# Second scores behind the even value product, its maximum ahead of the first scaling, even value rows copied in two parts

## Chip, core and metric

The kernel runs on one core of a Trainium2 chip. The metric is the device time of one execution in microseconds (us); three runs of the kernel before gave 957.9, 959.9 and 960.99, so the median is 959.9 us.

## What is computed

A sequence of 2048 rows of width 640 goes through an attention layer with a recurrent memory and then through a dense layer with a squared ReLU. The part that matters here is the attention. It walks over 64 segments of 32 rows; each segment needs the 8 memory rows that the segment before it left, so the segments can't run side by side:

```python
for s in range(n_seg):                       # 64 segments of 32 rows
    xs = x[:, s * seg_len:(s + 1) * seg_len, :]
    h = jnp.concatenate([mem, xs], axis=1)   # 8 memory rows + 32 rows
    q, k, v = (einsum('btd,dhe->bhte', h, W) for W in (Wq, Wk, Wv))   # 32 heads of 128
    scores = where(mask, einsum('bhqe,bhke->bhqk', q, k) * scale, -1e9)
    o = einsum('bhqk,bhke->bhqe', softmax(scores), v)
    o = einsum('bhte,hed->btd', o, Wo)
    mem = o[:, :M, :]                        # handed to the next segment
    outs.append(o[:, M:, :])
```

Around it stand a layer norm, the residual sums and the dense layer.

## The kernel before

The order of instructions on each engine is written out by hand; nothing is moved by a scheduler. One call of `step` is one segment, some 12 us long. Its order on TensorE (PE in the profile):

- The projections q (first 16 heads), k, q, k (second 16 heads), each 20 matmuls: `proj` (L234), 5 chunks of the 640 inputs times 4 column strips of the array, which run side by side. ScalarE (ACT) evacuates each result into a row tile (L253, L246, L482) and VectorE (DVE) turns it with 32 by 32 block transposes (L258, and L485 in two halves for the second k). GpSimd (POOL) spreads the queries of the memory rows into `qz` (L441, L443).
- `scores(0)` (L495): the memory rows' scores of the first 16 heads, 16 small matmuls into the bank `sm`. `soft1(0)` then takes the maximum on DVE (L501) and the exponential with its sum on ACT (L504, an activation and the reading of its accumulator).
- The value product has two halves of 512 columns, even (`ps0`) and odd (`ps1`). The even one runs in two pieces with `token_scores(0)` (L587) between them; ACT copies it out as 512 columns (L594).
- The odd product's first chunk (4 matmuls, in a bank of the three of the pool `mm`), then `soft2(0)`: reciprocal (L510), a product with the mask `same` (L511) and the scaling into `pm` (L515) on DVE. Then `scores(1)` and `soft1(1)`, the same for the second 16 heads, in the same bank `sm`. Then `soft3`: a transpose on DVE (L526) and four copies into `pB0` (L529), one on DVE, one on ACT, two on POOL.
- The rest of the odd product with `token_scores(1)` between its chunks, its copy by ACT (L608), and `soft2(1)` on DVE: reciprocal, product (L510, L511), the scaling with the mask `own` (L518), and the transpose into `pB1` (L521).
- Pieces of the other projections (`fill`: tail projections of later segments, 8 or 9 pieces of mostly 4 matmuls to a step, each group of 5 in a bank of `mm`) stand between the two value products of the memory rows: `values(0)` (L537, L542; reads `pB0` and the even value columns, writes the PSUM tile `po0`) and `values(1)` (reads `pB1` and the odd columns, writes `po1`).
- The output projection of the memory rows (`wo_rounds`, L270, 64 matmuls into `pw`), evacuated by ACT (L285, L286) and added by DVE (L287), and transposed into `hT` (L380): this is what the next segment's first projection waits for. Beside it run the rest of `fill` and the token values (L421, L426) of the segment before.

The PSUM has eight banks: three for `mm`, one for `chn` (`sm`, `pw`, one k), four for `po0` and `po1`; `potile(h)` hands out the first bank of `po0` or `po1` as a projection tile before the values use it. A tile of `em` (`bufs=1`) holds the exponentials, first those of the first half, then those of the second.

An instruction waits for signals of other engines. Where it and its weight load have to wait for more signals than they carry, a wait instruction of its own stands ahead of them in the engine's queue; the built program's order shows them.

Of the kernel before, what the change touches and what calls it, by code (L numbers as in the profile page):

```python
# [9 lines left out]
ALU = mybir.AluOpType  # L10
AX = mybir.AxisListType
F32 = mybir.dt.float32
BF16 = mybir.dt.bfloat16
# [3 lines left out]
def kernel(  # L17
# [16 lines left out]
    nc = tc.nc  # L34
# [3 lines left out]
    SEG = 32  # L38
    G = 4
    HG = H // G  # L40
# [8 lines left out]
    TL = SEG - HD  # L49
    NK = SEG + M  # L50
# [18 lines left out]
    s1 = ctx.enter_context(tc.tile_pool(name="s1", bufs=1))  # L69
    s2 = ctx.enter_context(tc.tile_pool(name="s2", bufs=2))  # L70
# [5 lines left out]
    wv = wts.tile([128, DC * HE], BF16)  # L76
# [14 lines left out]
    for g in range(G):  # L91
        r = slice(32 * g, 32 * g + 32)
# [4 lines left out]
    pBs = [const.tile([128, G, 2 * SEG], BF16, name="pB%d" % k) for k in range(2)]  # L97
# [43 lines left out]
    for q in range(4):  # L141
        nc.vector.tensor_copy(out=o0[32 * q:32 * q + 32, :].rearrange("m (c f) -> m c f", f=32),
                              in_=mem0[:].rearrange("m (c q f) -> m q c f", q=4, f=32)[:, q])
# [27 lines left out]
    def rows_of(b, sp):  # L171
        at = HD + sp * SEG
        return lambda c: hTs[b % 2][:, c * CW + at:c * CW + at + SEG]
# [50 lines left out]
    def proj(w, by, lhs, n, ps, c0, c1):  # L224

        if by == "columns":
            wr = w[:].rearrange("p (c g j n k e) -> p c n k g j e", c=DC, g=G, n=2, j=4, k=4)
        elif by == "half":
            wr = w[:].rearrange("p (c k j n e) -> p c n k j e", c=DC, k=G, n=2, j=4)
        else:  # L230
            wr = w[:].rearrange("p (c k n f) -> p c n k f", c=DC, k=G, n=2)
        for c in range(c0, c1):
            for k in range(4):
                nc.tensor.matmul(ps[32 * k:32 * k + 32, :], lhsT=lhs(c), rhs=wr[:, c, n, k], start=(c == 0), stop=(c == DC - 1))  # L234

    def mmtile():
        return mm.tile([128, 512], F32, tag="mm", name="ps")

    def potile(h):
        return pop.tile([128, 2, 512], F32, tag="po%d" % h, name="px%d" % h)[:, 0, :]  # L240
# [81 lines left out]
    def tail_units(b, which):  # L322
        w = {"q": wq, "k": wk, "v": wv}[which]
        lhs = lambda c: tail_rows(b, c)
        st = {}

        def unit(n, c):
            def f():
                if c == 0:
                    st[n] = mmtile()  # L330
                proj(w, "columns" if which != "v" else "order", lhs, n, st[n], c, c + 1)
                return (True, lambda: tail_out(b, which, n, st[n][:])) if c == DC - 1 else None
            return f
        return [unit(n, c) for n in range(2) for c in range(DC)]
# [117 lines left out]
    def step(b, sp, v=None):  # L452
        s = b * 4 + sp
        last = s == NS - 1
        lhs = rows_of(b, sp)
        ready = v is not None
        if not ready:
            v = s2.tile([128, EG], BF16, tag="v", name="v")
# [29 lines left out]
        sms, ems, zms = {}, {}, {}  # L488

        def scores(n):  # L490
            sm = chn.tile([128, 512], F32, tag="ch", name="sm")
            for j in range(4):
                for g in range(G):
                    p = n * 16 + g * 4 + j
                    nc.tensor.matmul(sm[32 * g:32 * g + 32, 0:NK], lhsT=qz[:, p, :], rhs=kT[:, p, :],  # L495
                                     start=(j == 0), stop=(j == 3), skip_group_check=True)
            sms[n] = sm

        def soft1(n):
            mx = s2.tile([128, 1], F32, tag="mx", name="mx")  # L500
            nc.vector.tensor_reduce(out=mx[:], in_=sms[n][:, 0:NK], op=ALU.max, axis=AX.X, negate=True)  # L501
            em = s2.tile([128, SEG + NK], BF16, tag="em", name="em", bufs=1)
            zm = s2.tile([128, 1], F32, tag="zm", name="zm")
            nc.scalar.activation(out=em[:, SEG:], in_=sms[n][:, 0:NK], func=ACT.Exp, bias=mx[:, 0:1], scale=1.0,  # L504
                                 accum_out=zm[:])
            ems[n], zms[n] = em, zm

        def soft2(n):
            rm = s2.tile([128, 1], F32, tag="rm", name="rm")
            nc.vector.reciprocal(out=rm[:], in_=zms[n][:])  # L510
            nc.vector.tensor_tensor(out=ems[n][:, 0:SEG].rearrange("p (j k) -> p j k", k=TL),  # L511
                                    in0=ems[n][:, 2 * SEG:].unsqueeze(1).to_broadcast([128, 4, TL]), in1=same[:], op=ALU.mult)
            if n == 0:
                pm = s1.tile([128, HG, TL], BF16, tag="pkt", name="pm")[:].rearrange("p i k -> p (i k)")
                nc.vector.tensor_scalar(out=pm, in0=ems[n][:, 0:2 * SEG], scalar1=rm[:, 0:1], scalar2=None, op0=ALU.mult)  # L515
                return pm
            pm = s1.tile([128, HG, 32], BF16, tag="pk", name="pm")[:].rearrange("p (g a) k -> p g (a k)", g=G)
            nc.vector.scalar_tensor_tensor(out=pm, in0=ems[n][:, 0:2 * SEG].unsqueeze(1).to_broadcast([128, G, 2 * SEG]),  # L518
                                           scalar=rm[:, 0:1], in1=own[:].unsqueeze(2).to_broadcast([128, G, 2 * SEG]),
                                           op0=ALU.mult, op1=ALU.mult)  # L520
            nc.vector.transpose(out=pBs[1][:], in_=pm)  # L521
            return pBs[1]

        def soft3(pm):
            pT = s1.tile([128, 2, 32], BF16, tag="pTt", name="pT")[:].rearrange("p u k -> p (u k)")
            nc.vector.transpose(out=pT, in_=pm)  # L526
            for g, copy in enumerate((nc.vector.tensor_copy, nc.scalar.copy, nc.gpsimd.tensor_copy, nc.gpsimd.tensor_copy)):
                r = slice(32 * g, 32 * g + 32)
                copy(out=pBs[0][r, g], in_=pT[r])  # L529
            return pBs[0]  # L530

        def values(n, pB, po):
            cols = po[:, 0, 0:128]
# [29 lines left out]
        def first_half():  # L563
            if not last:
                scores(0)
                soft1(0)
# [8 lines left out]
        if not ready:  # L575
            ps0 = potile(0)
# [6 lines left out]
        def token_scores(n):  # L583
            skv = view()
            for j in range(4):
                for g in range(G):
                    nc.tensor.matmul(skv[32 * g:32 * g + 32, n * 4 + j, :], lhsT=qT[:, n * 16 + g * 4 + j, :],  # L587
                                     rhs=kT[:, n * 16 + g * 4 + j, :], start=True, stop=True,
                                     skip_group_check=True)

        token_scores(0)
        if not ready:
            proj(wv, "half", lhs, 0, ps0, 2, DC)
            nc.scalar.copy(out=v[:, 0:512], in_=ps0[:])  # L594
            ps1 = mmtile()
            proj(wv, "half", lhs, 1, ps1, 0, 1)
        if not last:
            pm0 = soft2(0)
            scores(1)
            soft1(1)  # L600
            pT0 = soft3(pm0)
        if not ready:
            proj(wv, "half", lhs, 1, ps1, 1, 2)
        token_scores(1)
        if not ready:
            proj(wv, "half", lhs, 1, ps1, 2, DC)
        if not ready:
            nc.scalar.copy(out=v[:, 512:1024], in_=ps1[:])  # L608
        if not last:
            pT1 = soft2(1)  # L610
        def causal(skv):
            nc.vector.tensor_tensor(out=skv[:, :, M:NK], in0=skv[:, :, M:NK],
                                    in1=mask[:].unsqueeze(1).to_broadcast([128, HG, SEG]), op=ALU.add)
# [34 lines left out]
        ek = s1.tile([128, HG, NK], BF16, tag="ek", name="ek")  # L648
# [5 lines left out]
        pkt = s1.tile([128, HG, TL], BF16, tag="pkt", name="pkt")  # L654
# [28 lines left out]
        pTt = s1.tile([128, 2, 32], BF16, tag="pTt", name="pTt")  # L683
# [194 lines left out]
    for b in range(2, NB):  # L878
        for which in "qk":
            u = tail_units(b, which)  # L880
            plan += [(4 * b - 3 + (which == "k"), 4 * b - 5, u[DC * n:DC * n + DC]) for n in range(2)]
    for b in range(10, NB):
        u = tail_units(b, "v")
# [25 lines left out]
    for b in range(NB):  # L909
        for sp in range(4):  # L910
# [34 lines left out]
            if 2 <= e <= NK4 + 1:  # L945
                late.insert(0, (1.15, lambda e=e: prep_stats0(e - 2), b * 4 + sp))
                mid.append(lambda e=e: prep_norm0(e - 2))
            step(b, sp, v0 if b + sp == 0 else None)

    def end_tails():  # L950
# [14 lines left out]
    for t in range(S // NT):  # L965
# [8 lines left out]
        for fc in range(FC):  # L974
# [10 lines left out]
            r = rs_[fc % 4]  # L985
            nc.scalar.activation(out=r[:, 0:w], in_=ps[:, 0:w], func=ACT.Relu, bias=b1f[:, fc:fc + 1], scale=1.0)  # L986
            nc.vector.tensor_tensor(out=f1T[:, fc, 0:w], in0=r[:, 0:w], in1=r[:, 0:w], op=ALU.mult)
            if more and fc >= 1 and (fc - 1) // 3 < NK4:
                k, stage = divmod(fc - 1, 3)
# [30 lines left out]
        for q in range(NK4):  # L1020
# [6 lines left out]
            for hh in range(2):  # L1027
                k = pr + 2 * hh
# [44 lines left out]
```

## Time and profile before

| what | value |
|---|---|
| median of three runs | 959.9 us (957.9 to 960.99) |
| the profiled execution's own time | 956.46 us |
| its span, first to last instruction | 954.6 us, TensorE clock granted 0.998 |
| PE busy | 923.6 us (97%) |
| DVE, ACT, POOL busy | 703.6 (74%), 552.3 (58%), 309.5 (32%) |
| from 100 to 750 us | PE 641.87 of 650.00 us busy |
| chain that ended last | PE 80%, ACT 6%, DVE 5%, DMA 5%, SP queue 2% |

The segments lie between about 60 and 815 us. They repeat closely: measured from one even value copy (L594) to the next, most steps take 11.98 us, and seven take 12.17. A matmul's record has a tail after its last column has gone in (four strips of 512 columns take 0.38 us on record but follow each other every 0.215 us), so a busy PE is not a PE without stalls. A row of the timeline merges instructions of one kind that follow each other; the bracket tells how long the engine was idle before it and what ended that.

### The profile page before, as it was taken

How to read it: one execution, taken by the hardware profiler on the slowest of the kernel's cores; microseconds unless marked ns; L12 is line 12 of the kernel's file. 1: busy time of each engine (PE TensorE's matmuls, PEld its weight loads, DVE VectorE, ACT ScalarE, POOL GpSimd, SP SyncE). 2: the span in 40 equal slices, each digit the busy share in tenths (PEclk: the TensorE clock that was granted, in tenths of full speed). 3: DMA queues.
4: the chain of work that ended last, by engine and by line, in shares of the span. 5: the costliest groups of instructions: out<-in, count | busy, mean ns of one | idle time of the engine just before them, and what ended most of it. 6: DMA issues, size and time to landing. Idle time of an engine off the chain costs nothing.

```text
span 954.6 us, 55984 instructions
## 1 busy us (share of the span) xinstructions
PE 923.6 (97%) x24760; PEld 544.0 (57%) x24760; DVE 703.6 (74%) x2131; ACT 552.3 (58%) x1460; POOL 309.5 (32%) x1002
## 2 busy tenths in 40 slices
PE   5979999999999999999999999999999999999998
PEld 2445555655565656556565656565655555555555
DVE  5168888778877887877877787878787788556632
ACT  2546666666666666666666666666666666523321
POOL 2123333333333333333333333333333333353300
PEclk9999999999999999999999999999999999999999
DMA  9983201010101000100101010101010221633320
GB/s 352 402 265 70 38 18 27 16 30 13 23 20 28 16 21 24 21 25 11 34 17 23 14 31 14 32 12 33 8 32 8 54 43 21 203 108 88 94 56 28
DMA packets 65875, 56.66 MB, mean 59 GB/s; under 512 B 37384, under 2 KB 61712, under 8 KB 63712
## 3 DMA queue, kind: packets, MB, share of 16 engines
q1 hardware_dynamic: 65392, 52.74, 19.6%
q8 instruction: 194, 3.18, 1.4%
q14 instruction: 49, 0.40, 0.1%
q0 software_dynamic: 224, 0.33, 0.1%
q10 hardware_dynamic: 16, 0.01, 0.0%
HBM read 38.37 MB, written 9.44 MB: 50 GB/s over the span
## 4 chain that ended last, share of the span: by engine, by line
PE 80%; ACT 6%; DVE 5%; DMA 5%; SPq 2%; issue 1%; ACTq 0%
PE ps L234 23%; PE pw L270 15%; PE px L234 14%; PE pk L234 7%; PE y L1030 6%; PE ps L978 6%; ACT v L594 3%; PE ps L270 2%; DMA wq<-in_A_Wq_dram 2%; PE po L421 2%; ACT em L504 2%; SPq L151 2%; DVE pm L518 2%; PE po L537 2%; DVE pB L521 2%
## 5 line engine op out<-in xcount | busy, mean ns | idle before, releaser
L234 PEld LDWEIGHTS <-hT 128*32 128x32 bf16 x7680 | 178.9, 96 | 161.2 <-DVE hT L380 24.3
L270 PE MATMUL pw<-wo,oT 128*32 128x320 bf16 x4224 | 157.7, 299 | 2.5 <-DMA wo<-in_A_Wo_dram 1.0
L270 PEld LDWEIGHTS <-oT 128*32 128x32 bf16 x4224 | 120.0, 96 | 22.8 <-issue 3.7
L258 DVE STREAM_TRANSPOSE qT<-row 128x512 bf16<-128x512 bf16 x128 | 89.5, 699 | 44.1 <-ACT row L253 43.7
L234 PE MATMUL ps<-wv,hT 128*32 128x512 bf16 x1260 | 91.9, 377 | 0.0
L649 ACT ACTIVATE ek<-tk 128x320 bf16<-128x320 f32 x64 | 30.1, 470 | 101.9 <-DVE tk L644 101.9
L655 POOL TENSOR_TENSOR pkt<-ek,rk 128x64 bf16<-128x64 bf16 x64 | 18.8, 294 | 212.1 <-ACT otmp L286 176.0
L234 PE MATMUL px<-wv,hT 128*32 128x512 bf16 x1260 | 85.2, 377 | 0.0
L234 PE MATMUL ps<-wq,hT 128*32 128x512 bf16 x1260 | 81.3, 383 | 3.3 <-DVE hT L380 2.8
L234 PE MATMUL ps<-wk,hT 128*32 128x512 bf16 x1280 | 80.0, 379 | 0.0
L234 PE MATMUL px<-wq,hT 128*32 128x512 bf16 x1260 | 78.9, 379 | 0.0
L234 PEld LDWEIGHTS <-hTt 128*32 128x32 bf16 x1920 | 54.4, 97 | 42.2 <-issue 10.1
L234 PE MATMUL pk<-wk,hT 128*32 128x512 bf16 x1240 | 77.7, 379 | 0.0
L986 ACT ACTIVATE wv<-ps,b1f 128x512 bf16<-128x512 f32 (+1 forms) x56 | 37.6, 672 | 67.0 <-PE ps L978 66.5
L432 ACT CAST oT<-po 128x512 bf16<-128x512 f32 x128 | 68.7, 589 | 8.2 <-PE po L426 2.5
L441 POOL COPY qz<-qT 128x96 bf16<-128x96 bf16 x126 | 33.4, 265 | 111.4 <-DVE qT L258 111.4
L285 ACT COPY otmp<-pw 64x96 f32<-64x96 f32 (+2 forms) x129 | 28.8, 223 | 54.0 <-PE pw L270 33.4
L1030 PE MATMUL y<-wq,wk 128*128 128x320 bf16 x416 | 58.9, 299 | 0.2
L482 ACT CAST row<-ps 128x256 bf16<-128x256 f32 x126 | 40.7, 375 | 30.0 <-PE ps L234 29.1
L253 ACT ACTIVATE row<-ps 128x512 bf16<-128x512 f32 x93 | 54.8, 613 | 5.3 <-PE ps L234 4.0
L253 ACT ACTIVATE row<-px 128x512 bf16<-128x512 f32 x63 | 37.6, 597 | 32.2 <-PE px L234 32.2
L537 PEld LDWEIGHTS <-v 128*32 128x32 bf16 x2016 | 34.1, 94 | 34.7 <-issue 15.6
(138 smaller groups left out, 1886.1 us busy)
## 6 DMA issues: line engine op xcount, KB each, us to landing
wv<-in_A_Wv_dram SPq DMA_DIRECT2D x5, 1024.0 KB
wq<-in_A_Wq_dram SPq DMA_DIRECT2D x5, 1024.0 KB
wk<-in_A_Wk_dram SPq DMA_DIRECT2D x5, 1024.0 KB
wo<-in_A_Wo_dram SPq DMA_DIRECT2D x8, 640.0 KB
o_all<-o SPq DMA_DIRECT2D x256, 7.5 KB
vt<-vt_d SPq DMA_DIRECT2D x60, 64.0 KB
xt<-in_A_x_dram SPq DMA_DIRECT2D x19, 160.0 KB
wq<-in_B_w_dram SPq DMA_DIRECT2D x1, 2080.0 KB
```

Source lines behind the costliest of these rows:

```text
L234: nc.tensor.matmul(ps[32 * k:32 * k + 32, :], lhsT=lhs(c), rhs=wr[:, c, n, k], start=(c == 0), stop=(c == DC - 1))
L253: nc.scalar.mul(out=row, in_=ps, mul=scale)
L258: nc.vector.transpose(out=dst[:, n * 16:(n + 1) * 16, 0:32], in_=row.rearrange("p (h e) -> p h e", e=32))
L270: nc.tensor.matmul(pw[32 * j:32 * j + 32, c0:c0 + DH], lhsT=lhs(p), rhs=wov2[:, head(p), ch], start=(h == 0), stop=(h == 15))
L432: nc.scalar.copy(out=oTg[:, gs, :, :, 0:SEG], in_=po[1][h][:, :, 0:256].rearrange("p g (n j q) -> p g n j q", n=2, q=32))
L441: nc.gpsimd.tensor_copy(out=d.rearrange("p a (j f) -> p a j f", j=3)[:, :, :, 0:M], in_=src[:, :, 0:3, :])
L482: nc.scalar.copy(out=row[:, u * 256:(u + 1) * 256], in_=ps[:, u * 256:(u + 1) * 256])
L537: nc.tensor.matmul(cols[32 * k:32 * k + 32].rearrange("p (g i m) -> p i g m", g=G, i=4)[:, j], lhsT=v[:, i * E + 32 * k:i * E + 32 * k + 3 ...
L649: nc.scalar.activation(out=ek[:], in_=tk[:], func=ACT.Exp, scale=1.0)
L978: nc.tensor.matmul(ps[:], lhsT=w1[:, c, fc * 128:(fc + 1) * 128], rhs=hnT[:, c, :], start=(c == 0), stop=(c == DC - 1))
L986: nc.scalar.activation(out=r[:, 0:w], in_=ps[:, 0:w], func=ACT.Relu, bias=b1f[:, fc:fc + 1], scale=1.0)
L1030: nc.tensor.matmul(y[hh][:, 0:DH], lhsT=f1T[:, fc, k * 128:(k + 1) * 128], rhs=w2[:, fc, cs], start=(fc == 0 and not hf), stop=(fc == FFUL ...
```

## The change

Four things change for every segment but the first and the last. The 16 matmuls of `scores(1)` follow directly on the even value product; the odd product's first chunk, which stood before them, joins its second chunk behind them. The maximum of the second half (L501) stands ahead of the first half's scaling, which goes from `soft2` to `soft3`; the exponentials of the first half lie in the buffer of `ek`, no longer in that of the second half's. ACT copies the even value rows out in two parts of 256 columns, the first where the whole copy was, the second behind the exponential of `soft1(1)`. And the odd value product gets its bank from `potile(1)`, of `po1`, in place of one of the three of `mm`.

```diff
         def soft1(n):
...
-            em = s2.tile([128, SEG + NK], BF16, tag="em", name="em", bufs=1)
+            if n:
+                em = s2.tile([128, SEG + NK], BF16, tag="em", name="em", bufs=1)[:]
+            else:
+                em = s1.tile([128, HG, NK], BF16, tag="ek", name="em")[:].rearrange("p i k -> p (i k)")[:, 0:SEG + NK]
...
-            if n == 0:
-                pm = s1.tile([128, HG, TL], BF16, tag="pkt", name="pm")[:].rearrange("p i k -> p (i k)")
-                nc.vector.tensor_scalar(out=pm, in0=ems[n][:, 0:2 * SEG], scalar1=rm[:, 0:1], scalar2=None, op0=ALU.mult)
-                return pm
+            return rm
+
+        def soft3(rm):
+            pm = s1.tile([128, HG, TL], BF16, tag="pkt", name="pm")[:].rearrange("p i k -> p (i k)")
+            nc.vector.tensor_scalar(out=pm, in0=ems[0][:, 0:2 * SEG], scalar1=rm[:, 0:1], scalar2=None, op0=ALU.mult)
+            pT = s1.tile([128, 2, 32], BF16, tag="pTt", name="pT")[:].rearrange("p u k -> p (u k)")
+            nc.vector.transpose(out=pT, in_=pm)
+            for g in range(G):
+                r = slice(32 * g, 32 * g + 32)
+                (nc.vector.tensor_copy, nc.scalar.copy, nc.gpsimd.tensor_copy)[min(g, 2)](out=pBs[0][r, g], in_=pT[r])
+            return pBs[0]
...
             proj(wv, "half", lhs, 0, ps0, 2, DC)
-            nc.scalar.copy(out=v[:, 0:512], in_=ps0[:])
-            ps1 = mmtile()
-            proj(wv, "half", lhs, 1, ps1, 0, 1)
+            nc.scalar.copy(out=v[:, 0:256], in_=ps0[:, 0:256])
+            if last:
+                nc.scalar.copy(out=v[:, 256:512], in_=ps0[:, 256:512])
+            ps1 = potile(1)
+            if last:
+                proj(wv, "half", lhs, 1, ps1, 0, 1)
         if not last:
-            pm0 = soft2(0)
+            rm0 = soft2(0)
             scores(1)
             soft1(1)
-            pT0 = soft3(pm0)
+            if not ready:
+                nc.scalar.copy(out=v[:, 256:512], in_=ps0[:, 256:512])
+            pT0 = soft3(rm0)
         if not ready:
-            proj(wv, "half", lhs, 1, ps1, 1, 2)
+            proj(wv, "half", lhs, 1, ps1, int(last), 2)
         token_scores(1)
...
         if not last:
-            pT1 = soft2(1)
+            pT1 = soft4(soft2(1))
```

The scaling of the second half, its transpose and the four copies into `pB0` stay the same instructions on the same engines (`soft4` is the second half's part of the old `soft2`). The orders of POOL and of the DMA queue don't change. In the built program three waits become or stop being instructions of their own: the exponential of the second half carries its one wait itself; the transpose of `soft3` now has the wait for the scaling directly behind it; and the first matmul of `values(1)`, which waited for `pB1` itself, now has three signals to wait for (`pB1`, the odd copy, and the odd product in its bank), the first of them in a wait instruction ahead of its weight load, in all 62 steps.

More of the change, by code (lines that the diff above doesn't have):

```diff
@@ L512, in soft2, with soft4 @@
                                     in0=ems[n][:, 2 * SEG:].unsqueeze(1).to_broadcast([128, 4, TL]), in1=same[:], op=ALU.mult)
-            if n == 0:
-                pm = s1.tile([128, HG, TL], BF16, tag="pkt", name="pm")[:].rearrange("p i k -> p (i k)")
-                nc.vector.tensor_scalar(out=pm, in0=ems[n][:, 0:2 * SEG], scalar1=rm[:, 0:1], scalar2=None, op0=ALU.mult)
-                return pm
+            return rm
[8 more added lines that the diff above has]
+            return pBs[0]
+        def soft4(rm):
             pm = s1.tile([128, HG, 32], BF16, tag="pk", name="pm")[:].rearrange("p (g a) k -> p g (a k)", g=G)
-            nc.vector.scalar_tensor_tensor(out=pm, in0=ems[n][:, 0:2 * SEG].unsqueeze(1).to_broadcast([128, G, 2 * SEG]),
+            nc.vector.scalar_tensor_tensor(out=pm, in0=ems[1][:, 0:2 * SEG].unsqueeze(1).to_broadcast([128, G, 2 * SEG]),
                                            scalar=rm[:, 0:1], in1=own[:].unsqueeze(2).to_broadcast([128, G, 2 * SEG]),
@@ L522, in soft2 @@
             return pBs[1]
[L524 to L530, printed above, removed]
         def values(n, pB, po):
```

## The prediction

> **What bounds the kernel now.** I read the page, then the chain of waits for one plain step (160 to 172 us), then the timeline of DVE and PE for its middle, then the single records there. Every time below is of the step whose even value copy starts at 165.10 us. The chain, start, duration and owner:
>
> ```profile
> 165.10 0.59 ACT v L594
> ...
> 165.75 0.39 ACT em L504 x2
> ...
> 166.16 0.16 DVE rm L510
> ...
> 167.02 0.46 DVE pB L521
> ...
> 167.52 0.27 PE po L537 x16
> ```
>
> The reader is to see that the step's end runs through ACT and DVE, not PE, between 165.10 and 167.52: the second half's exponential, then reciprocal, product, scaling and transpose, then `values(1)`. From 167.52 on it is the output projection, the new memory rows and the next projections, PE with short hops. DVE in the same stretch:
>
> ```profile
> 164.23 0.77 DVE L485 STREAM_TRANSPOSE kT<-row 128x256 bf16<-128x256 bf16 x2
> ...
> 165.45 0.20 DVE L501 TENSOR_REDUCE mx<-sm 128x1 f32<-128x40 f32 x1
> 165.57 0.23 DVE L526 STREAM_TRANSPOSE pT<-pm 128x64 bf16<-128x64 bf16 x1
> 165.84 0.17 DVE L529 COPY pB<-pT 32x64 bf16<-32x64 bf16 x1
> 166.16 0.16 DVE L510 RECIPROCAL rm<-zm 128x1 f32<-128x1 f32 x1 [0.16 <-ACT em L504]
> ```
>
> Here: the second k's transposes end at 165.00, and DVE idles only 0.16 us, before the reciprocal. PE:
>
> ```profile
> 165.09 0.27 PE L495 MATMUL sm<-kT,qz 128*32 128x40 bf16 x16
> ...
> 166.75 0.60 PE L234 MATMUL ps<-wk,hTt 128*32 128x512 bf16 x8
> 167.52 0.27 PE L537 MATMUL po<-pB,v 128*32 128x32 bf16 x16 [0.17 <-DVE pB L521]
> ```
>
> Two groups of 0.215 from 166.75 end at 167.18, so PE really stands 0.34 us before `values(1)`. In 48 of 62 steps `values(1)` starts like this, 2.42 us after L594; the step after L594 then takes the same 9.56 us or more. So the step's length moves with the start of `values(1)`, one to one. In seven steps it starts at 2.60 instead: a fill group after `values(0)` opens a bank that the odd copy still holds. The list of waits from 100 to 750 us has it:
>
> ```profile
> PE ps L234 <- ACT v L608: 2.4, 11, 0.2
> ```
>
> **The change part by part.**
>
> *Second scores earlier.* The four matmuls at 164.88 no longer stand before them, which would be 0.215 us. But the third of the 16 needs the second k's last transpose, which ends at 165.00, so PE can go on at 165.05 and not at 164.88. One step of before shows PE waiting exactly there:
>
> ```profile
> 67.69 0.77 DVE L485 STREAM_TRANSPOSE kT<-row 128x256 bf16<-128x256 bf16 x2 [0.41 <-ACT row L482]
> ...
> 68.85 0.20 DVE L501 TENSOR_REDUCE mx<-sm 128x1 f32<-128x40 f32 x1
> ```
>
> ```profile
> 68.28 0.51 PE L495 MATMUL sm<-kT,qz 128*32 128x40 bf16 x16
> ```
>
> The transposes end at 68.46, the scores stretch to 0.51 us, and the maximum starts 0.39 after the transposes. So the maximum comes at 165.00 + 0.39 = 165.39, 0.06 earlier, not 0.215. The other 0.17 is a new PE stall; it shortens the 0.34 before `values(1)` and costs nothing while that lasts.
>
> *Maximum ahead of the scaling, on DVE.* The scaling follows the maximum as the transpose did, 0.12 behind its start (165.45 to 165.57): 165.51, and takes 0.24 (row L515): 165.75. The transpose now waits for the instruction just in front of it, through a wait of its own. Direct, such a pair has 0.035 between (product to scaling, 0.035 in 63 of 63); with a wait of its own 0.11 (transpose to copy in the first step, 54.00 to 54.12). I take 0.11, the row of that case: transpose 165.86 to 166.09. DVE's copy 0.035 later, 166.13 to 166.30. Before, it ended at 166.01: DVE's part is now 0.29 later, because the scaling used to lie in the time in which DVE waited for the scores.
>
> *Exponential earlier on ACT.* The split copy frees ACT after 0.37 (row L482, 256 columns) at 165.47; the maximum ends at 165.59, and the exponential carries its wait itself, so it starts at about 165.62 and its sum is there at 166.00, against 166.13. That is in time for a reciprocal that DVE reaches at 166.22 (0.08 before the copy's end, as L510 does at 164.92 behind L485). So ACT's part of the chain is gone and **DVE is late next**. The product starts 0.04 behind (164.92 to 164.96): 166.26, where before it stood at 166.25. Gain and loss cancel. If the reciprocal can't overlap the copy, it starts at 166.31 and the product, 0.08 behind and with the longer reciprocal of 0.16, at 166.41: 0.15 worse.
>
> *Product beside POOL.* It took 0.22 at 166.25, beside POOL's two copies (165.94, 0.51 in all), and 0.15 in the first two steps, where it started under 0.02 after POOL's second copy. POOL's copies follow the transpose by 0.13, so the first now starts at 166.22 or 166.23, 0.03 ahead of the product. I take 0.22; 0.15 is the other end. The Trainium skill (SBUF — State Buffer, Who interferes with whom) says that a Vector instruction with two SBUF inputs and a GpSimd read exclude each other, whoever comes first; the two lengths agree with it. By that rule the second scaling too meets a POOL copy, which ends at 166.73, long before the scaling's 0.48 would.
>
> From the product on nothing changes: `pB1` is transposed at 167.48 (167.47 before); 167.41 with the short product.
>
> *The added wait on PE.* `values(1)` now passes a wait instruction for `pB1`, then loads weights, then multiplies; queued behind it are `values(1)` and the output projection. Before, weights were loaded and the matmul started 0.054 after the transpose. The price of a wait that holds: at the step of 68 us the scores have such a wait for the first half of the transposes, which ended at 68.137, and the first matmul started at 68.284: 0.147. So + 0.09; bounds 0 and 0.12. It has no cover.
>
> *Four copies, even copy's second part.* ACT: sum read 166.03, second part to 166.40, `pB0` copy to 166.67, odd copy to 167.28 (0.58). POOL's end is 166.73, so `values(0)` goes from 166.59 to 166.78. Then 0.16, two fill groups 0.43: 167.37, still before `values(1)`; cover left 0.25. If DVE were faster, this would bind next.
>
> *Bank of the odd product.* The wait for L608 goes. In the seven steps there are three fill groups: 166.78 + 0.16 + 0.645 = 167.59, so the new wait binds there too, at 167.62 against 167.70.
>
> *Sum.* Per plain step: + 0.01 (chain) + 0.09 (wait) = + 0.10, so `values(1)` at 167.62. 48 x 0.10 = + 4.8; seven steps x - 0.08 = - 0.6; of the other seven steps I count four at + 0.10: + 0.4. Together + 4.6 us. Against the profiled execution 956.46 + 4.6 = 961.1; the runs' median lies 3.4 higher, so I forecast 959.9 + 4.6 = **964.5**.
>
> **The rivals.**
>
> *No overlap on DVE*, chance 0.15. The reciprocal waits for the copy's end: + 0.25 a step. For it: the copies of 32 partitions at 5.25 us follow each other with 0.013 between, not overlapped. Against: the first of them, on partitions 0 to 31 as here, started 0.08 before its forerunner's end. 48 x 0.25 + 7 x 0.07 + 4 x 0.25 = + 13.5: 973. The Trainium skill (VectorE: DVE Perf Modes, The DRAIN you can't avoid) says that the next op doesn't start before the pipe is empty, which would make this sure; L510 at 164.92 against an end of 165.00 shows otherwise here. The same page (Two Vector instructions with no wait between them) holds back only instructions that start in another quarter of the partitions, which speaks for the overlap.
>
> *POOL loses the race*, chance 0.2: product 0.15, `values(1)` at 167.55, + 0.03: 48 x 0.03 - 7 x 0.11 (fill binds at 167.59) + 0.1 = + 0.8: 960.7, no change.
>
> *Faster*, chance 0.13: the separate waits cost nothing, on DVE (0.035 in place of 0.11) and PE (0 in place of 0.09), because both queues take them early. Then `pB1` is there 0.065 earlier: 48 x - 0.065 = - 3.1, the seven steps to 167.51, - 1.3: - 4.5, 955.4. It decides where both waits together cost under about 0.09 of my 0.165. Against it: both prices are from rows where the wait held. The full intended gain (scores 0.215 earlier) is excluded by the transposes' end.
>
> *The bank wait doesn't go* would add 0.6 to the forecast; no case of its own.
>
> **How the numbers follow.** Forecast 0.52, the others 0.15, 0.2, 0.13. 0.3% (2.9 us) is about what a measurement of this kernel can tell from no change. Slower: 0.45 of the forecast's 0.52, all of no overlap, 0.02 of the race: 0.62. Same: 0.07 + 0.18 = 0.25. Faster 0.13. The range leaves out the faster rival and reaches from a little under the lost race to no overlap: 958.5 to 973.5.
>
> **What would show it.** In the profile after: second scores stretched to about 0.5 us; their maximum 0.39 after L485's end; no idle DVE before the second reciprocal; `values(1)` 0.15 after the transpose of `pB1` and 2.52 after the even copy's start; a common step of 12.08 us; no wait of PE for the odd copy. Wrong would make it: an idle DVE there again, or `values(1)` 0.05 after the transpose.

## The result, and the profile after

The changed kernel takes 964.18 us in the median of six runs (963.13 to 965.79); the kernel before took 959.8 in six runs on the same chip (957.9 to 960.99). The ratio is 1.0049, with a 95% interval of 1.0035 to 1.0062: slower, by 4.4 us. The profiled execution took 963.13 us at a granted clock of 0.998.

The step whose first half of the even value copy starts at 129.46 us is a common one (12.09 us to the next; the commonest length of a step is 12.10 after the change and was 11.98 before it). The timeline of DVE:

```profile
128.58 0.77 DVE L485 STREAM_TRANSPOSE kT<-row 128x256 bf16<-128x256 bf16 x2
...
129.74 0.20 DVE L501 TENSOR_REDUCE mx<-sm 128x1 f32<-128x40 f32 x1 [0.27 <-PE sm L495]
129.86 0.23 DVE L520 TENSOR_SCALAR pm<-em,rm 128x64 bf16<-128x64 bf16 x1
130.19 0.24 DVE L522 STREAM_TRANSPOSE pT<-pm 128x64 bf16<-128x64 bf16 x1
130.47 0.17 DVE L525 COPY pB<-pT 32x64 bf16<-32x64 bf16 x1
130.56 0.14 DVE L513 RECIPROCAL rm<-zm 128x1 f32<-128x1 f32 x1
130.64 0.20 DVE L514 TENSOR_TENSOR em<-em,same 128x32 bf16<-128x32 bf16 x1
130.87 0.50 DVE L530 SCALAR_TENSOR_TENSOR pm<-em,rm,own 128x256 bf16<-128x256 bf16 x1
131.40 0.45 DVE L533 STREAM_TRANSPOSE pB<-pm 128x256 bf16<-128x256 bf16 x1
```

The bracket that names what DVE was idle for has moved: before the change it stood at the second reciprocal, which waited for ACT; now it stands at the maximum, 0.27 us, which waits for the second scores. The scaling (L520), which used to fill that gap, stands behind the maximum. From there DVE has no idle time that is booked to another engine. The timeline of PE:

```profile
129.23 0.45 PE L495 MATMUL sm<-kT,qz 128*32 128x40 bf16 x16
...
131.30 0.73 PE L270 MATMUL ps<-wo,oTt 128*32 128x320 bf16 x16
131.99 0.27 PE L541 MATMUL po<-pB,v 128*32 128x32 bf16 x16
```

The second scores start 0.22 us earlier against the even copy than before, and stretch from 0.27 to 0.45, since they wait in their middle for the last transpose of the second k (129.35). `values(1)` starts at 131.99: 0.14 after the transpose of `pB1` ends (131.85), and 2.53 after the even copy's start. The list of waits of PE from 100 to 750 us has no wait for the odd copy any more; of `values(1)` and `values(0)` it shows only

```profile
PE po L541 <- POOL pB L525: 0.2, 1, 0.2
PE po L541 <- DVE pB L533: 0.2, 1, 0.2
```

And the chain of waits now gives the whole stretch to PE:

```profile
131.48 0.54 PE ps L270 x16
132.02 0.24 PE po L541 x15
```

Read alone this says that PE is the bound. It isn't: the last fill group's tail of 0.3 us lies over a stall. A record of 0.73 us of four groups with a tail of 0.30 means that a group starts every 0.14 us ((0.73 - 0.30) / 3), so PE could start the next work 0.56 us after 131.30; in a later experiment `values(1)` does follow the same groups after 0.55. Here it is 0.69. The real stall is shorter than before the change, since the fill groups stand later too: in the same step of before, the last of these groups starts at + 2.03 and `values(1)` at + 2.42, here they start at + 2.24 and + 2.53. The record's tail covers what is left of it, so no bracket shows it; to see a stall on PE, compare starts.

### The profile page after: what moved, and what is told of

Read it like the earlier page. It is cut to its first block, busy times and chain, and to the rows that moved or that the text cites. A ratio compares the mean times of both kernels' runs of the same rounds, so it can differ in the third digit from the quotient of the medians.

```text
span 961.3 us, 56112 instructions
## 1 busy us (share of the span) xinstructions
PE 932.2 (97%) x24749; PEld 542.8 (56%) x24760; DVE 697.3 (73%) x2131; ACT 559.5 (58%) x1523; POOL 312.0 (32%) x1002
## 4 chain that ended last, share of the span: by engine, by line
PE 88%; DMA 5%; DVE 2%; SPq 2%; issue 1%; POOL 1%; ACT 1%; DVEq 0%; POOLq 0%
PE ps L234 22%; PE px L234 20%; PE pw L270 15%; PE pk L234 7%; PE y L1039 6%; PE ps L987 6%; PE ps L270 3%; PE sm L495 2%; PE po L541 2%; DMA wq<-in_A_Wq_dram 2%; PE po L421 2%; SPq L151 2%; PE ps L591 1%; DMA wo<-in_A_Wo_dram 1%; PE po L546 1%
## 5 line engine op out<-in xcount | busy, mean ns | idle before, releaser
L234 PEld LDWEIGHTS <-hT 128*32 128x32 bf16 x7680 | 176.0, 96 | 152.9 <-DVE hT L380 22.1
L234 PE MATMUL px<-wv,hT 128*32 128x512 bf16 x2520 | 170.9, 377 | 0.0
L525 POOL COPY pB<-pT 32x64 bf16<-32x64 bf16 x126 | 30.1, 239 | 82.7 <-DVE pT L522 78.7
L495 PEld LDWEIGHTS <-qz 128*32 128x32 bf16 x2016 | 34.9, 94 | 38.0 <-POOL qz L443 14.8
```

## The experiments

They were measured on three chips (e1 to e4, e5 to e8, e9 to e11), each group beside the kernel before, whose medians there were 958.4 to 958.7 us; ratios are to the median of the same chip. The table gives, from the start of the even copy, when the transpose of `pB1` ends and when `values(1)` starts in a common step, and where `values(1)` starts in the seven steps that waited for the bank (2.60 before).

| kernel | `pB1` transposed | `values(1)` | in the seven | ratio, 95% |
|---|---|---|---|---|
| before | 2.37 | 2.42 | 2.60 | 1 |
| after | 2.39 | 2.53 | 2.53 to 2.58 | 1.0049 (1.0035 to 1.0062) |
| e1 after, odd product in `mm` | 2.39 | 2.45 | 2.73 to 3.03 | 1.0059 (1.0036 to 1.0082) |
| e2 before, bank alone | 2.37 | 2.51 | 2.51 | 1.0064 (1.0041 to 1.0086) |
| e3 after, spare matmul | 2.39 | 2.45 | 2.50 to 2.55 | 1.0028 (1.0012 to 1.0045) |
| e4 after, early scaling | 2.17 | 2.32 | 2.32 to 2.37 | 0.9958 (0.994 to 0.9975) |
| e5 both e3 and e4 | 2.17 | 2.24 | 2.30 to 2.34 | 0.992 (0.9902 to 0.9938) |
| e6 after, one even copy | 2.39 | 2.53 | 2.53 to 2.58 | 1.0051 (1.0033 to 1.0068) |
| e7 e4, one even copy | 2.17 | 2.32 | 2.31 to 2.36 | 0.9945 (0.9927 to 0.9963) |
| e8 e5, first chunk back | 2.24 | 2.29 | 2.37 | 0.9911 (0.9888 to 0.9933) |
| e9 before, own buffer | 2.24 | 2.29 | 2.56 in five, 3.12 and 3.28 | 0.9932 (0.9912 to 0.9951) |
| e10 before, buffer, bank, spare | 2.24 | 2.29 | 2.29 | 0.9923 (0.9903 to 0.9943) |
| e11 before, bank, spare | 2.37 | 2.42 | 2.42 | 0.9951 (0.9932 to 0.997) |

My theory after the result: the loss is the wait instruction ahead of `values(1)` (W in the expectations), and no gain shows because DVE, with the scaling behind the maximum, has become the late engine (D).

**The wait instruction: e1, e2, e3, e11.** e1 takes the bank back in the changed kernel:

```diff
-            ps1 = potile(1)
+            ps1 = mmtile()
```

> The change with the odd value product back in a bank of the pool mm; all else as changed. Theory W (the cost is the added wait instruction in front of the odd values): the wait instruction is gone, the odd values start 0.05 and not 0.15 us after the transpose of pB1, the common step is 12.01 us (12.10 with the change, 11.98 before). The seven steps with three fill groups wait again for the odd copy, which now ends at 2.04: 2.09 + 0.645 = 2.74, a step of 12.30. Sum against before: 48 x 0.02 + 7 x 0.14 + 0.1 = + 2.0, ratio 1.002. Rival D (the cost is the order on DVE and the copies, the wait is free): as the change, ratio 1.005 or more.

Measured: 963.04 us, 1.0059, which by the time alone speaks against W. The records agree with W: `values(1)` starts at 2.45, 0.06 after the transpose. What I had counted too low is the bank wait, now that ACT has four copies. The odd copy ends at 2.04 instead of 1.91, and three fill groups follow it in the seven steps; I had 2.74 there, and they start at 2.73 to 3.03. In other steps too a fill group starts 0.05 after the odd copy's end, and in several of these `values(1)` starts at 2.52 to 2.71. Over all steps its starts sum to 4.4 us more than before, where the expectation had 2.0. A step of e1 in which it ended at 244.88 us:

```profile
244.62 0.24 PE L546 MATMUL po<-pB,vt 128*32 128x128 bf16 x4
244.93 0.83 PE L234 MATMUL ps<-wq,hTt 128*32 128x512 bf16 x12
245.57 0.27 PE L541 MATMUL po<-pB,v 128*32 128x32 bf16 x15
```

The group starts 0.05 after the copy, `values(1)` 0.64 behind: 2.74 where the kernel before had 2.60. So this run has two changes of opposite sign and doesn't settle the price by its time. e2 makes the bank change alone, in the kernel before:

```diff
-            ps1 = mmtile()
+            ps1 = potile(1)
```

> The kernel before with one part of the change, the odd value product in po1's bank. Theory W: the wait instruction comes with the bank, the odd values start 0.15 after the transpose, + 0.09 in 48 steps, - 0.08 in seven: + 4.0, ratio 1.004, common step 12.07. Rival D: the bank alone costs nothing and the bank wait goes: - 1.3, ratio 0.999.

Measured: 964.46 us, 1.0064. Nothing else is changed, and the whole loss is there. By the records it is less than by the time: the starts of `values(1)` sum to 3.7 us more than before, near the 4.0 expected, and the medians lie 5.8 apart. The DVE and PE timelines of e2:

```profile
134.03 0.45 DVE L521 STREAM_TRANSPOSE pB<-pm 128x256 bf16<-128x256 bf16 x1
```

```profile
134.62 0.28 PE L537 MATMUL po<-pB,v 128*32 128x32 bf16 x16 [0.17 <-DVE pB L521]
```

The transpose ends at 134.48, `values(1)` starts 0.14 later; before it was 0.05. e3 keeps the bank in the changed kernel and gives two of the three signals to another instruction, ahead of `values(1)` and of little work:

```diff
+            nc.tensor.matmul(po[1][1][0:32, 0, 256:264], lhsT=v[:, 512:544], rhs=pBs[0][:, 0, 0:8],
+                             start=True, stop=True, skip_group_check=True)
             values(1, pT1, po[1][1])
```

> The change with one more matmul of 8 columns into unused columns of po1 in front of the odd values; it takes the waits for the odd copy and for the bank, so that the odd values' first matmul waits for pB1 alone and needs no wait instruction. Adds work that no output uses. Theory W: odd values 0.05 after the transpose, common step 12.01, the seven steps bound by fill at 2.48: + 0.02 x 48 - 0.12 x 7 + 0.1 = + 0.2, ratio 1.000. Rival D: as the change, 1.005.

Measured: 960.56 us, 1.0028, between the two. `values(1)` is at 2.45, not back at 2.42, since DVE is 0.02 later than before, and in about half of the steps it starts later still, in most of these at 2.47 to 2.61; over all steps its starts sum to 2.1 us more than before. e11 puts the same line into e2:

> The kernel before with the odd product in the bank of po1 and the spare matmul. Theory W (all that the bank brings is the wait instruction, + 0.09, against the bank waits, - 0.18 in seven steps): values(1) back at 2.42, seven steps at 2.42 to 2.44 in place of 2.60: - 1.2, ratio about 0.999; beside 1.0064 of the bank alone. Rival (the bank itself costs, by sharing po1 with the values): 1.004 or more.

Measured: 953.59 us, 0.9951. The same step as above:

```profile
130.59 0.45 DVE L521 STREAM_TRANSPOSE pB<-pm 128x256 bf16<-128x256 bf16 x1
```

```profile
130.84 0.17 PE L636 MATMUL po<-pB,v 128*32 128x8 bf16 x1
131.09 0.28 PE L537 MATMUL po<-pB,v 128*32 128x32 bf16 x16
```

131.04 to 131.09: 0.05 again. Between e2 and e11 there is only the line that moves waits, and it is worth 1.1%. W holds for the place and the price on the chain; but it expected 0.999, and this run is faster than that by more than its interval (below).

**DVE as the late engine: e4, e5.** e4 puts the first half's scaling back ahead of the second maximum, in the changed kernel:

```diff
-            rm0 = soft2(0)
+            pm0 = scale0(soft2(0))
...
-            pT0 = soft3(rm0)
+            pT0 = soft3(pm0)
```

(`scale0` holds the scaling's two lines of `soft3`.)

> The change with the first half's scaling back ahead of the second half's maximum (it lies in the time in which DVE waits for the scores, and its transpose needs no separate wait in sequence). If DVE is the late engine after the change, as predicted: transpose at 0.40 after the even copy in place of 0.74, reciprocal at 0.94 bound by ACT's sum, pB1 at 2.17 in place of 2.39, odd values at 2.32 behind their wait instruction, 2.45 in the seven steps: 48 x -0.10 - 7 x 0.15 = - 5.9, ratio 0.994, common step 11.88. If ACT or PE bound the chain: as the change, 1.005.

Measured: 952.66 us, 0.9958. The timeline of DVE in e4, in a step whose even copy starts at 130.52:

```profile
130.57 0.24 DVE L520 TENSOR_SCALAR pm<-em,rm 128x64 bf16<-128x64 bf16 x1
130.80 0.20 DVE L501 TENSOR_REDUCE mx<-sm 128x1 f32<-128x40 f32 x1
130.92 0.24 DVE L525 STREAM_TRANSPOSE pT<-pm 128x64 bf16<-128x64 bf16 x1
...
131.45 0.16 DVE L513 RECIPROCAL rm<-zm 128x1 f32<-128x1 f32 x1
131.53 0.16 DVE L514 TENSOR_TENSOR em<-em,same 128x32 bf16<-128x32 bf16 x1
```

The maximum starts at + 0.28, as in the changed kernel: the scaling fits into the 0.27 that DVE waits for the scores. Against the even copy, the transpose of `soft3` is 0.33 earlier than in the changed kernel, the reciprocal 0.17, the end of the transpose of `pB1` 0.22. So the new order on DVE gains nothing and costs 0.22 us a step. e5 has both repairs:

> The changed kernel with the first scaling ahead of the second maximum, and with the spare matmul that takes the waits for the odd copy and the bank ahead of values(1) (it multiplies into columns of po1 that nothing reads). If the two repairs add up on the chain (theory W: the wait instruction costs 0.09 us once in a step), the transpose of pB1 ends at 2.17 and values(1) could start at 2.22; the fill groups before it then let PE start at 2.24, so 0.08 a step is gained on early scaling alone: ratio about 0.992, values(1) at 2.24 with a gap to the transposes of 0.07. If PE is already the limit at 2.32 (rival P), nothing is gained on early scaling alone: 0.996.

Measured: 951.18 us, 0.992, as W expected. PE in e5:

```profile
132.36 0.73 PE L270 MATMUL ps<-wo,oTt 128*32 128x320 bf16 x16
132.90 0.17 PE L648 MATMUL po<-pB,v 128*32 128x8 bf16 x1
132.91 0.28 PE L544 MATMUL po<-pB,v 128*32 128x32 bf16 x16
```

Here `values(1)` follows the fill groups 0.55 after their start; this is PE without a stall.

**Which part of the rest does anything: e6 to e10.** e6 and e7 take the even copy in one part again, in the changed kernel and in e4:

```diff
-            nc.scalar.copy(out=v[:, 0:256], in_=ps0[:, 0:256])
+            nc.scalar.copy(out=v[:, 0:512], in_=ps0[:])
...
-                nc.scalar.copy(out=v[:, 256:512], in_=ps0[:, 256:512])
```

> The changed kernel with the even value rows copied by ACT in one part, as before the change. Theory D (DVE is the late engine there): the sum of the exponential comes about 0.13 later, at 1.03, still before DVE is free of its copy for the second reciprocal (1.10), so values(1) stays at 2.53 and the ratio at 1.005. Rival S (the split carries part of the chain): the reciprocal follows the sum by some 0.10 and starts at 1.13 or later; values(1) at 2.56 or more, ratio 1.007 or more.

> The first scaling ahead of the second maximum, and the even copy in one part. Theory D: with DVE early, ACT is late again: the sum comes at about 1.03, the reciprocal at 1.06 in place of 0.93, the product meets POOL's first copy and takes 0.20 in place of 0.16, so values(1) moves from 2.32 to about 2.49 and the ratio from 0.996 to about 1.004. Rival S' (the split is worth nothing in either order): 0.996.

Measured: 963.53 us, 1.0051, and 953.16 us, 0.9945. The first as D expected, but by a wrong reason, as the second shows, which was a miss: the split is worth nothing in either order. ACT's timeline in e6:

```profile
129.66 0.58 ACT L598 CAST v<-px 128x512 bf16<-128x512 f32 x1 [0.35 <-PE px L234]
130.17 0.29 ACT L507 ACTIVATE em<-sm,mx 128x40 bf16<-128x40 f32 x1
```

The exponential starts at 130.17, 0.07 before the copy in front of it ends (130.24), and as early as with the split copy (+ 0.51). It waits for the maximum, not for the copy. e8 puts the odd product's first chunk back ahead of the second scores, in e5:

```diff
-            if last:
-                proj(wv, "half", lhs, 1, ps1, 0, 1)
+            proj(wv, "half", lhs, 1, ps1, 0, 1)
...
-            proj(wv, "half", lhs, 1, ps1, int(last), 2)
+            proj(wv, "half", lhs, 1, ps1, 1, 2)
```

> Both repairs, and the odd product's first chunk back ahead of the second scores. Theory T (the second k's last transpose holds the scores, so that going ahead of the chunk gains only some 0.06 of the 0.215): the maximum starts at 0.35 in place of 0.28, the transpose of pB1 ends at 2.24 in place of 2.17, values(1) at 2.29 in place of 2.24; ratio about 0.9945 beside 0.992 of both repairs alone. Rival (moving the scores is worth its four matmuls): values(1) 0.2 later, ratio 1.001 or more. Rival (it is worth nothing): the same ratio as both repairs alone.

Measured: 949.59 us, 0.9911. On the chain the records show what theory T says, 0.07 on the transpose (2.24 and 2.17) and 0.05 on `values(1)`. In the time this can't be told from nothing: the intervals of e5 and e8 overlap, and e8 is the lower one. e9 does only one thing to the kernel before, giving the first half's exponentials the buffer of `ek`:

```diff
-            em = s2.tile([128, SEG + NK], BF16, tag="em", name="em", bufs=1)
+            if n:
+                em = s2.tile([128, SEG + NK], BF16, tag="em", name="em", bufs=1)[:]
+            else:
+                em = s1.tile([128, HG, NK], BF16, tag="ek", name="em")[:].rearrange("p i k -> p (i k)")[:, 0:SEG + NK]
```

> The kernel before, with one thing of the change: the exponentials of the first half lie in the buffer of ek, nothing is moved. Theory B (the buffer is the part of the change that shortens the chain): the second exponential no longer has to wait for the first scaling, so it carries its wait for the maximum itself and starts 0.06 earlier (0.58 in place of 0.64 after the even copy's start); reciprocal at 1.00 in place of 1.06; the product then starts ahead of POOL's second copy and takes 0.155 in place of 0.22; transpose of pB1 ends at 2.24 in place of 2.37, values(1) at 2.29 in place of 2.42. The seven steps that wait for the bank stay at 2.60. 48 x -0.13: ratio about 0.9935. Rival (the gain of early scaling came from the second scores ahead of the chunk): ratio 0.999 to 1.001.

Measured: 951.9 us, 0.9932. ACT and DVE in e9 (even copy at 128.83):

```profile
129.41 0.29 ACT L507 ACTIVATE em<-sm,mx 128x40 bf16<-128x40 f32 x1
```

```profile
129.83 0.16 DVE L513 RECIPROCAL rm<-zm 128x1 f32<-128x1 f32 x1
129.91 0.16 DVE L514 TENSOR_TENSOR em<-em,same 128x32 bf16<-128x32 bf16 x1
...
130.62 0.45 DVE L524 STREAM_TRANSPOSE pB<-pm 128x256 bf16<-128x256 bf16 x1
```

The exponential at + 0.58 instead of 0.65, the reciprocal at + 1.00 instead of 1.06, the product 0.16 long instead of 0.22: together 0.13. This is what was worth doing in the change. e10 joins the three parts that help, own buffer, bank and spare matmul, in the order of the kernel before:

> The kernel before, with the own buffer of the first exponentials, the odd product in the bank of po1, and the spare matmul ahead of values(1); second scores, order on DVE and the even copy in one part as before the change. Theory B + W: values(1) at 2.29, and the seven steps no longer at 2.60 but at 2.29 to 2.37: 48 x -0.13 - 7 x 0.25 = -8: ratio about 0.991, the same as both repairs, with two of the four parts of the change left away. Rival (the moved scores or the split carry part of it): 0.994 or more.

Measured: 951.03 us, 0.9923. In the profiled execution `values(1)` starts at 2.29 to 2.31 in nearly all steps, and the seven are among them. The first 61 steps, from one even copy to the next, take 728.7 us together, where they take 738.1 before and 744.1 after. e5, e8, e9 and e10 can't be told apart by time; all four beat both kernels. e10 leaves two of the four parts away, and that it is better than e9 alone is shown by the records only (2.29 in the seven steps).

## Why the prediction was right, point by point

*Second scores.* Right: the maximum starts 0.39 after the end of the k transposes (129.35 to 129.74), so 0.07 is gained against the even copy and not 0.215; the scores took 0.45 where I said some 0.5. e8 against e5 shows the same 0.07 in another order of DVE.

*Maximum ahead of the scaling.* Right in its lengths: scaling 0.12 behind the maximum, 0.10 and not 0.035 to the transpose, DVE's copy at + 1.01 (1.03 forecast). The prediction named the reason, the scaling used to lie in the time in which DVE waited for the scores; e4 shows it, and gives the price: 0.22 us a step on the transpose of `pB1`.

*Exponential earlier on ACT.* The time was right, the sum there at + 0.90, but this step gave a wrong cause: "The split copy frees ACT". e6 shows the exponential just as early behind the whole copy. What brings it forward is the earlier maximum and, as e9 shows, the own buffer, without which a separate wait instruction stands ahead of the exponential. The prediction named that too, but it did not work out that this alone would be worth 0.13 a step.

*Product beside POOL.* 0.20 at + 1.18, forecast 0.22 at + 1.16; both end at + 1.38. Here it starts 0.07 behind the start of a POOL copy; before the change it started 0.04 behind one and took 0.22. In e4 and e9, where it starts 0.03 and 0.02 ahead of one, it takes 0.16. The Trainium skill (SBUF — State Buffer, Who interferes with whom) states that such a product and a GpSimd read exclude each other; 0.16, 0.20 and 0.22, by which of the two started first and how long before, agree with that.

*The added wait.* Right: 0.14 to 0.15 from the transpose to `values(1)`, against 0.05. e2 and e11 differ in the line that moves the waits alone and lie 1.1% apart, 10.9 us. The 0.09 us in 61 steps make 5.5 of them. So the price on the chain is settled, and about half of what the line is worth in time is not explained by it.

*Split even copy.* `values(0)` starts at 1.68, as forecast. The split itself gains nothing, neither in the order of the change (e6) nor with DVE early (e7), where by the prediction's cause it should have.

*Bank.* The mechanism was right: the wait is gone. The prediction counted seven steps and set them off against the longer wait (- 0.6); the seven gained 0.02 to 0.07 each, 0.4 together. The list of waits of before has 12 waits for the odd copy, 2.6 us, and that of e11 has none: it is 4.8 us faster (2.9 to 6.5) where 1.2 was expected. Of that the starts of `values(1)` show 1.7 us, net of three steps that came later, which is near the forecast. The rest is not shown to be the bank's. The profiled executions have single steps that are longer than the common one, and their excess sums to 7.3 us in before, its bank waits included, and to 3.6 in e11, but to 7.8 in e2, which has the same bank as e11. Three of the pauses in before are booked to `issue` (0.3, 0.3 and 0.2 us), which means that PE waited for nothing that the profile shows. Why e11 has so few long steps is open.

*Sum.* Forecast + 0.10 a common step; measured + 0.11 on `values(1)` and + 0.12 on the step (11.98 to 12.10). Forecast + 4.6, measured + 4.4 between the medians. That these lie 0.2 apart is in part luck: in the two profiled executions the starts of `values(1)` sum to + 5.5 over 61 steps, and the steps to + 6.0, so the medians also hold differences that no term of the forecast stood for. By the experiments the + 0.11 of a common step is made of: own buffer - 0.13 (e9), moved scores - 0.07 (2.24 to 2.17, e8 and e5), order on DVE + 0.22 (e4), wait instruction + 0.09 (e2, e11), split 0 (e6): + 0.11. So the two gains of the change were there, and the new order on DVE took both back.

*The rivals.* No overlap on DVE: excluded, the reciprocal starts at 130.56, 0.08 before the copy in front of it ends. POOL loses the race: the product took 0.20, not 0.15. Faster, with both separate waits free: they cost 0.07 and 0.09.

## What to carry to other kernels

Before moving an instruction ahead of another on a busy engine, look at what lies in that engine's idle time now: an instruction that filled a wait costs nearly its whole length once it stands behind it (0.22 of 0.24 us here). Count signals, not only work: a third signal on an instruction at the end of a chain turned a direct wait of 0.05 us into one of 0.14 here, and a small instruction ahead of it that takes the signals known to be early removes that. The chain of waits gave the stall to PE because a matmul's tail covered it, so compare starts of the same groups between kernels.

## What the runs showed that I had not expected

ACT starts an exponential of 40 columns 0.07 us before the 512-column copy in front of it ends (130.17 against 130.24 in e6), so cutting a copy to let a small instruction through brought nothing.

A shared buffer of one tile cost 0.13 us a step without any line of the list of waits that names the buffer; DVE's wait before the reciprocal stood there for the exponential (8.6 us in 54 steps). Its price was a wait instruction on ACT (0.06), and the product's falling beside a POOL copy (0.07).

The first even copy, ahead of which these kernels hold nearly the same program, starts anywhere from 68.2 to 71.7 us in the profiled executions, as much as the effects studied here. I have not looked for its cause; times of one execution were therefore compared by steps, and kernels by medians.
